# Attention and feed-forward in one kernel: exponentials spread over more slots and tiles, GpSimd's weight work in pieces, one product kept in PSUM

## The chip, the cores and the metric

One NeuronCore of one Trainium2 chip runs the whole kernel. The metric is the device time of one execution in microseconds (us), the median of several runs. "PE" is TensorE, "PEld" its weight loads, "DVE" VectorE, "ACT" ScalarE, "POOL" GpSimd, "SP" the engine whose queue issues the DMAs.

## What is computed

```python
scores = 0.125 * q @ k.T                       # 4 batches, 8 heads, 768 positions, head size 64
keep = (key < n_sink) | ((0 <= query - key) & (query - key < window))   # 4 sinks, window 128
a = softmax(where(keep, scores, -1e9))         # sum + 1e-9 under the fraction
x = (a @ v) laid out as 3072 tokens x 512
h = x @ w_in                                   # 512 -> 2048
g = s * relu(h)**2 + b
out = g @ w_out                                # 2048 -> 512
```

All inputs and the output are float32. `w_in` and `w_out` are drawn with larger factors, so plain bfloat16 isn't used for the products. The kernel splits most operands of its matmuls into a high and a low part of a rounded float32 kind (`float32r`, one pass of TensorE), and multiplies hi by hi, hi by lo and lo by hi.

## The kernel before, in words

The 3072 tokens are eight chunks of 384 (`ORDER`, `CH`). A chunk's attention gives `x`, 512 x 384, as a high and a low tile; its feed-forward part (`moe_steps`) has 16 first products `l1(f)` (L589, 12 matmuls into one PSUM bank `h`) and 16 second ones `l2(f)` (L608, 9 matmuls into three banks `po` that stand through the chunk). While chunk c does its feed-forward, the attention of chunk c+1 is laid between its steps: `slots` are spread evenly over `steps` (last loop of the function). After `l1`, four instructions make `g`: ACT's relu (L592) from PSUM to `r`, DVE's `s*h*r` (L594), ACT's `+ b` rounded to the high part (L596), DVE's low part (L597).

Chunks 0 and 1 are computed by the class `Plain` ("chains" in plain float32), four head pairs each: `scores` (matmuls L491, DVE's mask and maximum L506, ACT's exponential L508, tiles `sm`), `norm` (DVE L513, L514 and six L519, times one over the sum), `turned` in three parts (four transposes each, L531, copied out by ACT, L533), `values` (matmuls L542, copies L544, L545). `plain_slots` puts them into slots: pair `pr` begins at slot 6 pr, `norm` comes `FN` slots later, `turned` `FB`, `values` `FC`; the first number of each holds for chunk 1, the second for chunk 0. Chunk 0 has nothing beside it but the making of weights: it is the kernel's head. Its tiles `sm0` are 8 (`E0`), four for a pair; chunk 1's are taken in turn from three tags of two tiles each.

Weights come as float64 words (1 MB for one f). `make_weight` turns them into float32 parts: ACT L211, L212, DVE L213, L214, GpSimd's add L216, ACT's rounding L220, and the low part L225 on GpSimd for odd f and on DVE for even f. In the head the first pieces are made; in chunk 0's feed-forward `before(f)` makes two more pieces ahead of each `l1(f)`. From chunk 1 on all weights stand in SBUF.

The instructions of an engine don't keep the order of the text. The program's builder orders them anew for each engine by what it takes to be ready (in the trace L149, of a later function, stands ahead of L117); on the chip each engine then runs its own list in order. PSUM has five banks in the pool `psA` (`sc`, `tp` of chunk 1, `o`, `h`) and three in `psO` (`po`, and `tp` of chunk 0). The other chunks' attention (`attn_slots`) uses two tiles `psks`, which `constants2` sets to zero.

Of the kernel before, what the change touches and what calls it, by code (L numbers as in the profile page):

```python
# [6 lines left out]
F32 = mybir.dt.float32  # L7
# [8 lines left out]
P = 128  # L16
# [15 lines left out]
WARM0 = 14  # L32
NARROW, NEARLY = 2, 8
RB, VB = 2, 2
E0 = 8
FN, FB, FC = (4, 2), (6, 6), (9, 10)
LB, LC, LD, L2 = 3, 6, 2, 2


# [1 line left out]
def tile_kernel(ctx, tc, qT, kT, k0, v, vsk, n_sink, window, w, s, b, out):  # L41
# [91 lines left out]
    def constants2():  # L133

        spread = wk.tile([P, P], F32, tag="y", name="spread", bufs=1)
        nc.gpsimd.memset(spread, 0.0)
        for j in range(2):
            nc.gpsimd.affine_select(
                out=spread[96:P].rearrange("p (a d) -> p a d", a=2), in_=spread[96:P].rearrange("p (a d) -> p a d", a=2),
                pattern=[[1, 2], [0, D]], compare_op=ALU.not_equal, fill=1.0, base=2 * j, channel_multiplier=-1)  # L140
        nc.scalar.copy(sel, spread)
        for t in psks:
            nc.gpsimd.memset(t, 0.0)

        nc.vector.tensor_tensor(out=tmp[:, :NS], in0=low[:, :NS], in1=snk[:, :NS], op=ALU.mult)
        nc.vector.tensor_tensor(out=tmp[:, :NS], in0=snk[:, :NS], in1=tmp[:, :NS], op=ALU.subtract)
        nc.vector.scalar_tensor_tensor(out=tm2[:, :NS], in0=rel1[:, :NS], scalar=w_ap, in1=snk[:, :NS],
                                       op0=ALU.is_ge, op1=ALU.mult)
        nc.vector.tensor_scalar(out=split[:, 0, :], in0=rel, scalar1=0.0, scalar2=None, op0=ALU.is_gt)  # L149
        nc.vector.tensor_scalar(out=split[:, 1, :], in0=rel, scalar1=0.0, scalar2=None, op0=ALU.is_le)  # L150
        mask(m_0[:, :NS], tmp[:, :NS])
        mask(m_1[:, 2 * P:], tm2[:, :NS])
        mask(m_even[:, P:P + NS], snk[:, :NS])
        cp = nc.gpsimd.tensor_copy
        upm, lom = m_full[2][:, P:2 * P], m_full[2][:, 2 * P:]
        cp(out=m_0[:, NS:], in_=lom)
        for m, l0 in ((m_1, P), (m_even, P + NS), (m_odd, P)):
            cp(out=m[:, :P], in_=upm)
            cp(out=m[:, l0:l0 + P], in_=lom)
        cp(out=m_odd[:, 2 * P:], in_=m_even[:, P:P + NS])  # L160
# [33 lines left out]
    def piece(f, j, t):  # L194

        n = len(raws[f])
        if n == 1:
            return weight[f][:, :, t, :]
        a = DM * 2 // n
        return weight[f][:, j * 2 // n, t, j * a % DM:j * a % DM + a]  # L200

    def make_weight(j):

        f = j // 2
        if j % 2 == 0 and f < NF:
            for i, raw in enumerate(raws[f]):
                lo, hi = raw[..., 0], raw[..., 1]
                t = scratch(f, i)  # L210
                nc.scalar.activation(lo, lo.bitcast(U32), AF.Copy, scale=2.0 ** -29)  # L211
                nc.scalar.mul(hi.bitcast(F32), hi.bitcast(F32), 2.0 ** -111)  # L212
                nc.vector.tensor_scalar(out=t, in0=hi, scalar1=3, scalar2=None, op0=ALU.logical_shift_left)  # L213
                nc.vector.scalar_tensor_tensor(out=hi, in0=hi, scalar=-0x80000000, in1=t,  # L214
                                               op0=ALU.bitwise_and, op1=ALU.bitwise_or)
                nc.gpsimd.tensor_tensor(out=hi, in0=hi, in1=lo, op=ALU.add)  # L216
        if j % 2 == 1:
            weight[f] = place(f).bitcast(F32R)
            for c, raw in enumerate(raws[f]):
                nc.scalar.copy(piece(f, c, 0), raw[..., 1].bitcast(F32))  # L220
        f -= 1
        if j % 2 == 0 and f >= 0:
            for c, raw in enumerate(raws[f]):
                e = nc.gpsimd if f % 2 == 1 else nc.vector
                e.tensor_tensor(out=piece(f, c, 1), in0=raw[..., 1].bitcast(F32), in1=piece(f, c, 0).bitcast(F32), op=ALU.subtract)  # L225
            raws.pop(f)


# [214 lines left out]
    class Plain:  # L443
# [33 lines left out]
        def scores(self, pr, group):  # L477
# [14 lines left out]
            for i in self.groups[group]:  # L492
                c0, n = (0, P, 0)[i], (i + 1) * P
                for hh in range(2):
                    j = 2 * (i // 2) + hh
                    if pp.sm[j] is None:
                        if self.c:
                            tag = ("kh", "kl", "qs")[self.turn % 3]
                            self.turn += 1
                            pp.sm[j] = wk.tile([P, CH], F32, tag=tag, name="smf")  # L500
                        else:
                            pp.sm[j] = first.tile([P, CH], F32, tag="sm0", name="sm0", bufs=E0)
                    sm = pp.sm[j][:, c0:c0 + n]
                    u = (self.c * H + 2 * pr + hh) * BLK + i
                    uu = slice(u, u + 1)
                    nc.vector.tensor_tensor_reduce(out=sm, in0=banks[(i // 2, hh)][:, c0:c0 + n], in1=m_full[i], scale=-0.125, scalar=BIG,  # L506
                                                   op0=ALU.add, op1=ALU.min, accum_out=negm[:, uu])
                    nc.scalar.activation(sm, sm, AF.Exp, bias=negm[:, uu], scale=-1.0, accum_out=pp.z[:, 0, i, hh:hh + 1])  # L508
# [41 lines left out]
    def plain_slots(c):  # L550
# [6 lines left out]

        first_one = c == 0
        for pr in range(H // 2):
            t = 6 * pr  # L560
            at(t - (0 if first_one else 6), k.load, pr)
            for g in range(len(k.groups)):
                at(t + 2 * g, k.scores, pr, g)
            for part in range(3):
                at(t + FB[first_one] + part, k.turned, pr, part)
            at(t + FN[first_one], k.norm, pr)
            at(t + FC[first_one], k.values, pr)
# [10 lines left out]
    def moe_steps(x, store, wk, before=None, last=False):  # L578
# [3 lines left out]
        def l1(f):  # L582
# [4 lines left out]
            for cc in range(NCC):  # L587
                for wi, xi in ((0, 0), (0, 1), (1, 0)):
# [2 lines left out]
            r = wk.tile([P, CH], F32, tag="r", name="r", bufs=RB)  # L591
            nc.scalar.activation(r, h[:, :CH], AF.Relu, scale=1.0 / WUP)  # L592

            nc.vector.scalar_tensor_tensor(out=r, in0=h[:, :CH], scalar=sw_ap, in1=r, op0=ALU.mult, op1=ALU.mult)  # L594
            gg = wk.tile([P, 2, CH], F32R, tag="g", name="g", bufs=3)
            nc.scalar.activation(gg[:, 0, :], r, AF.Identity, bias=b_ap, scale=1.0)  # L596
            nc.vector.scalar_tensor_tensor(out=gg[:, 1, :], in0=r, scalar=b_ap, in1=gg[:, 0, :].bitcast(F32),  # L597
                                           op0=ALU.add, op1=ALU.subtract)
            g[f] = gg

# [141 lines left out]
    NC_ = 2 * B  # L742
    k, slots = plain_slots(0)
    k.load_first(slice(0, 1))
    nc.sync.dma_start(sb[:, 0:1], s.partition_broadcast(P))
    nc.sync.dma_start(sb[:, 1:2], b.partition_broadcast(P))
    constants()
    k.load_first(slice(1, NCC))
    k.load_values()
    for i, f in enumerate(slots):  # L750
        f()
        if i == 10:
# [7 lines left out]
    late_cm = tc.tile_pool(name="late", bufs=1)  # L760
    late.append(late_cm.__enter__())
    for c in range(NC_):
        steps = moe_steps(k.x, store_at(c), wk, before if c == 0 else None, c == NC_ - 1)
        slots = []
        if c + 1 < NC_:
# [59 lines left out]
```

## Time and profile before

| | us |
|---|---|
| median of 3 runs (lowest, highest) | 745.1 (744.76, 747.49) |
| profiled execution, its own time | 745.48 |
| its span, first to last instruction | 743.7 |
| busy: PE, PEld | 707.4 (95%), 617.5 (83%) |
| busy: DVE, ACT, POOL | 507.5 (68%), 478.7 (64%), 398.2 (54%) |
| mean granted TensorE clock | 0.977 of full speed |

The span is cut into stretches by the windows view; within one, the waits view says who waited for whom, and the timeline gives single instructions. Busy shares over the whole span mix stretches that are unlike each other.

### The profile page before, as it was taken

How to read it: one execution, taken by the hardware profiler on the slowest of the kernel's cores; microseconds unless marked ns; L12 is line 12 of the kernel's file. 1: busy time of each engine (PE TensorE's matmuls, PEld its weight loads, DVE VectorE, ACT ScalarE, POOL GpSimd, SP SyncE). 2: the span in 40 equal slices, each digit the busy share in tenths (PEclk: the TensorE clock that was granted, in tenths of full speed). 3: DMA queues.
4: the chain of work that ended last, by engine and by line, in shares of the span. 5: the costliest groups of instructions: out<-in, count | busy, mean ns of one | idle time of the engine just before them, and what ended most of it. 6: DMA issues, size and time to landing. Idle time of an engine off the chain costs nothing.

```text
span 743.7 us, 11974 instructions
## 1 busy us (share of the span) xinstructions
PE 707.4 (95%) x3848; PEld 617.5 (83%) x3848; DVE 507.5 (68%) x1213; ACT 478.7 (64%) x1169; POOL 398.2 (54%) x641
## 2 busy tenths in 40 slices
PE   6788799999999999999999999999999999999996
PEld 3367577789888998899888998899889999889885
DVE  6779999647874778657776678838776568743231
ACT  4978877567774777656774677738675578643222
POOL 2254654358982789626772589816664379710000
PEclk8889989999999999999999999999999999999999
DMA  7845131042221211111111222112111212001001
GB/s 272 339 169 191 33 115 57 27 126 67 62 65 44 70 56 53 44 64 50 54 49 49 73 67 67 46 40 64 55 52 41 86 42 61 9 1 43 1 0 48
DMA packets 27222, 53.03 MB, mean 71 GB/s; under 512 B 3472, under 2 KB 15376, under 8 KB 25232
## 3 DMA queue, kind: packets, MB, share of 16 engines
q1 hardware_dynamic: 27152, 52.18, 21.0%
q8 instruction: 33, 0.54, 0.3%
q14 instruction: 37, 0.30, 0.1%
HBM read 45.88 MB, written 6.29 MB: 70 GB/s over the span
## 4 chain that ended last, share of the span: by engine, by line
PE 67%; DVE 15%; ACT 6%; DMA 4%; issue 3%; POOL 3%; SPq 1%; ACTq 0%; DVEq 0%; POOLq 0%
PE po L608 29%; PE h L589 28%; PE o L376 2%; DVE g L597 2%; DMA vf<-in_v 2%; PE sc L303 2%; PE sc L304 2%; ACT sm L314 2%; DMA w<-in_w 2%; DVE w L214 2%; PE sc L324 2%; DVE wt L213 1%; POOL w L216 1%; DVE r L594 1%; DVE xm L385 1%
## 5 line engine op out<-in xcount | busy, mean ns | idle before, releaser
L589 PE MATMUL h<-x,w 128*128 128x384 f32 x1536 | 296.2, 342 | 3.5 <-DVE hl L343 2.5
L608 PE MATMUL po<-w,g 128*128 128x512 f32 x1152 | 293.2, 400 | 0.0
L589 PEld LDWEIGHTS h<-x,w 128*128 128x128 f32 x1536 | 268.7, 189 | 10.6 <-DVE hl L343 2.9
L608 PEld LDWEIGHTS po<-w,g 128*128 128x128 f32 x1152 | 211.8, 190 | 45.1 <-issue 2.4
L594 DVE SCALAR_TENSOR_TENSOR r<-h,sb,r 128x384 f32<-128x384 f32 x128 | 78.7, 615 | 68.9 <-ACT r L592 67.9
L597 DVE SCALAR_TENSOR_TENSOR g<-r,sb,g 128x384 fp32r<-128x384 f32 x128 | 92.0, 719 | 42.5 <-ACT g L596 41.5
L596 ACT ACTIVATE g<-r,sb 128x384 fp32r<-128x384 f32 x128 | 78.6, 614 | 52.1 <-DVE r L594 51.8
L340 POOL TENSOR_TENSOR hl<-two,hl 128x256 fp32r<-128x256 f32 x128 | 99.4, 777 | 20.8 <-ACT hl L339 18.1
L592 ACT ACTIVATE r<-h 128x384 f32<-128x384 f32 x128 | 62.5, 489 | 66.2 <-PE h L589 65.8
L314 ACT ACTIVATE sm<-sm,negm 128x272 f32<-128x272 f32 (+1 forms) x144 | 73.1, 508 | 45.7 <-DVE negm L308 43.4
L317 POOL TENSOR_TENSOR sm<-sm 128x128 f32<-128x128 f32 x128 | 65.4, 511 | 57.1 <-ACT sm L314 55.2
L308 DVE CUSTOM_DVE_ANT_0 sm<-sc,msk 128x272 f32<-128x272 f32 (+1 forms) x144 | 60.5, 420 | 47.7 <-PE sc L304 46.2
L284 POOL TENSOR_TENSOR kl<-kraw,kh 128x544 fp32r<-128x544 f32 (+1 forms) x48 | 62.5, 1303 | 24.5 <-ACT kh L282 23.9
L289 POOL TENSOR_TENSOR vv<-vraw,vv 128x256 fp32r<-128x256 f32 (+1 forms) x48 | 39.1, 816 | 38.3 <-ACT vv L288 38.0
L216 POOL TENSOR_TENSOR w<-w 128x1024 int32<-128x1024 int32 (+1 forms) x17 | 32.6, 1920 | 45.6 <-DVE w L214 25.1
L318 POOL COPY psk<-sm 128x48 f32<-128x48 f32 x144 | 40.7, 282 | 29.6 <-ACT sm L314 27.3
L337 DVE TENSOR_TENSOR two<-sc,split 128x256 f32<-128x256 f32 x128 | 53.4, 417 | 2.1 <-POOL hl L340 1.1
L339 ACT CAST hl<-two 128x256 fp32r<-128x256 f32 x128 | 50.2, 392 | 6.2 <-DVE two L337 6.2
L303 PE MATMUL sc<-kh,qs 128*128 128x272 f32 (+1 forms) x144 | 50.8, 355 | 0.0
L385 DVE TENSOR_TENSOR xm<-o,y 64x512 f32<-64x512 f32 x48 | 33.1, 689 | 24.1 <-ACT y L384 14.9
L376 PE MATMUL o<-hl,vv 128*128 128x256 f32 (+1 forms) x256 | 44.4, 275 | 0.0
L283 DVE TENSOR_TENSOR qs<-qraw,qs 64x384 fp32r<-64x384 f32 x48 | 38.3, 798 | 5.1 <-ACT qs L279 3.8
(129 smaller groups left out, 915.0 us busy)
## 6 DMA issues: line engine op xcount, KB each, us to landing
w<-in_w SPq DMA_DIRECT2D x15, 1024.0 KB, 9.1
kraw<-in_kT SPq DMA_DIRECT2D x32, 272.0 KB, 2.6
out<-ot SPq DMA_DIRECT2D x24, 256.0 KB, 2.0
qraw<-in_qT SPq DMA_DIRECT2D x24, 192.0 KB, 2.5
vraw<-in_v SPq DMA_DIRECT2D x16, 256.0 KB, 2.6
kraw<-in_kT SPq DMA_DIRECT2D x16, 208.0 KB, 2.4
vsraw<-in_vsk SPq DMA_DIRECT2D x24, 64.0 KB, 1.9
vraw<-in_v SPq DMA_DIRECT2D x8, 192.0 KB, 2.4
```

Source lines behind the costliest of these rows:

```text
L284: nc.gpsimd.tensor_tensor(out=hd.kl[:, :kw], in0=hd.k[:, :kw], in1=hd.kh[:, :kw].bitcast(F32), op=ALU.subtract)
L303: nc.tensor.matmul(sc[:, :n], hd.qs[:, qs], hd.kh[:, c0:c0 + n], start=True, stop=False)
L308: nc.vector.tensor_tensor_reduce(out=sm[:, :n], in0=sc[:, :n], in1=m, scale=-0.125, scalar=BIG, op0=ALU.add, op1=ALU.min, accum_out=negm[: ...
L314: nc.scalar.activation(sm[:, :n], sm[:, :n], AF.Exp, bias=negm[:, uu], scale=-1.0, accum_out=pp.zz[:, i, hh:hh + 1])
L317: nc.gpsimd.tensor_tensor(out=sm[:, c1:c1 + P], in0=sm[:, p1:p1 + P], in1=sm[:, c1:c1 + P], op=ALU.add)
L340: nc.gpsimd.tensor_tensor(out=lo, in0=both, in1=hi.bitcast(F32), op=ALU.subtract)
L589: nc.tensor.matmul(h[:, :CH], weight[f][:, 0, wi, cc * P:(cc + 1) * P], x[xi][:, cc, :], start=(i == 0), stop=(i == 11))
L592: nc.scalar.activation(r, h[:, :CH], AF.Relu, scale=1.0 / WUP)
L594: nc.vector.scalar_tensor_tensor(out=r, in0=h[:, :CH], scalar=sw_ap, in1=r, op0=ALU.mult, op1=ALU.mult)
L596: nc.scalar.activation(gg[:, 0, :], r, AF.Identity, bias=b_ap, scale=1.0)
L597: nc.vector.scalar_tensor_tensor(out=gg[:, 1, :], in0=r, scalar=b_ap, in1=gg[:, 0, :].bitcast(F32), op0=ALU.add, op1=ALU.subtract)
L608: nc.tensor.matmul(po[tb], gg[:, gi, tsl], weight[f][:, 1, wi, :], start=(f == 0 and i == 0), stop=(f == NF - 1 and i == 2))
```

## The change

The diff, whole. `E0` becomes 16, so each pair of chunk 0 has tiles of its own. `in_parts` issues a GpSimd operation in pieces of at most 256 columns; it is used for L216 and for L225 on GpSimd. The slot numbers become `FN` (3, 2), `FB` (7, 8), `FC` (11, 12), and chunk 1's pairs begin 5 slots apart and load 5 slots ahead. Chunk 1's exponentials take a fourth kind of tile, the two `psks`, which are therefore set to zero only when chunk 1's feed-forward begins. In chunk 0 (`before` is given) L594 writes back into `h`'s bank, and L596 and L597 read it there. In the head the second pair's q and k are loaded by themselves, and the loads of s and b come after the values.

```diff
--- before.py
+++ after.py
@@ -32,8 +32,9 @@
 WARM0 = 14
 NARROW, NEARLY = 2, 8
 RB, VB = 2, 2
-E0 = 8
-FN, FB, FC = (4, 2), (6, 6), (9, 10)
+E0 = 16
+PART = 256
+FN, FB, FC = (3, 2), (7, 8), (11, 12)
 LB, LC, LD, L2 = 3, 6, 2, 2
 
 
@@ -139,9 +140,6 @@
                 out=spread[96:P].rearrange("p (a d) -> p a d", a=2), in_=spread[96:P].rearrange("p (a d) -> p a d", a=2),
                 pattern=[[1, 2], [0, D]], compare_op=ALU.not_equal, fill=1.0, base=2 * j, channel_multiplier=-1)
         nc.scalar.copy(sel, spread)
-        for t in psks:
-            nc.gpsimd.memset(t, 0.0)
-
         nc.vector.tensor_tensor(out=tmp[:, :NS], in0=low[:, :NS], in1=snk[:, :NS], op=ALU.mult)
         nc.vector.tensor_tensor(out=tmp[:, :NS], in0=snk[:, :NS], in1=tmp[:, :NS], op=ALU.subtract)
         nc.vector.scalar_tensor_tensor(out=tm2[:, :NS], in0=rel1[:, :NS], scalar=w_ap, in1=snk[:, :NS],
@@ -199,6 +197,14 @@
         a = DM * 2 // n
         return weight[f][:, j * 2 // n, t, j * a % DM:j * a % DM + a]
 
+    def in_parts(out, in0, in1, op):
+
+        n = out.shape[-1]
+        for c in range(out.shape[1] if len(out.shape) == 3 else 1):
+            for a in range(0, n, PART):
+                q = (slice(None),) + ((c,) if len(out.shape) == 3 else ()) + (slice(a, min(a + PART, n)),)
+                nc.gpsimd.tensor_tensor(out=out[q], in0=in0[q], in1=in1[q], op=op)
+
     def make_weight(j):
 
 
@@ -213,7 +219,7 @@
                 nc.vector.tensor_scalar(out=t, in0=hi, scalar1=3, scalar2=None, op0=ALU.logical_shift_left)
                 nc.vector.scalar_tensor_tensor(out=hi, in0=hi, scalar=-0x80000000, in1=t,
                                                op0=ALU.bitwise_and, op1=ALU.bitwise_or)
-                nc.gpsimd.tensor_tensor(out=hi, in0=hi, in1=lo, op=ALU.add)
+                in_parts(hi, hi, lo, ALU.add)
         if j % 2 == 1:
             weight[f] = place(f).bitcast(F32R)
             for c, raw in enumerate(raws[f]):
@@ -221,8 +227,8 @@
         f -= 1
         if j % 2 == 0 and f >= 0:
             for c, raw in enumerate(raws[f]):
-                e = nc.gpsimd if f % 2 == 1 else nc.vector
-                e.tensor_tensor(out=piece(f, c, 1), in0=raw[..., 1].bitcast(F32), in1=piece(f, c, 0).bitcast(F32), op=ALU.subtract)
+                do = in_parts if f % 2 == 1 else nc.vector.tensor_tensor
+                do(out=piece(f, c, 1), in0=raw[..., 1].bitcast(F32), in1=piece(f, c, 0).bitcast(F32), op=ALU.subtract)
             raws.pop(f)
 
 
@@ -495,9 +501,9 @@
                     j = 2 * (i // 2) + hh
                     if pp.sm[j] is None:
                         if self.c:
-                            tag = ("kh", "kl", "qs")[self.turn % 3]
+                            tag = ("kh", "kl", "qs", "")[self.turn % 4]
+                            pp.sm[j] = wk.tile([P, CH], F32, tag=tag, name="smf") if tag else psks[self.turn // 4 % 2].rearrange("p i c -> p (i c)")
                             self.turn += 1
-                            pp.sm[j] = wk.tile([P, CH], F32, tag=tag, name="smf")
                         else:
                             pp.sm[j] = first.tile([P, CH], F32, tag="sm0", name="sm0", bufs=E0)
                     sm = pp.sm[j][:, c0:c0 + n]
@@ -557,8 +563,8 @@
 
         first_one = c == 0
         for pr in range(H // 2):
-            t = 6 * pr
-            at(t - (0 if first_one else 6), k.load, pr)
+            t = (6 if first_one else 5) * pr
+            at(t - (0 if first_one else 5), k.load, pr)
             for g in range(len(k.groups)):
                 at(t + 2 * g, k.scores, pr, g)
             for part in range(3):
@@ -591,10 +597,11 @@
             r = wk.tile([P, CH], F32, tag="r", name="r", bufs=RB)
             nc.scalar.activation(r, h[:, :CH], AF.Relu, scale=1.0 / WUP)
 
-            nc.vector.scalar_tensor_tensor(out=r, in0=h[:, :CH], scalar=sw_ap, in1=r, op0=ALU.mult, op1=ALU.mult)
+            hr = h[:, :CH] if before else r
+            nc.vector.scalar_tensor_tensor(out=hr, in0=h[:, :CH], scalar=sw_ap, in1=r, op0=ALU.mult, op1=ALU.mult)
             gg = wk.tile([P, 2, CH], F32R, tag="g", name="g", bufs=3)
-            nc.scalar.activation(gg[:, 0, :], r, AF.Identity, bias=b_ap, scale=1.0)
-            nc.vector.scalar_tensor_tensor(out=gg[:, 1, :], in0=r, scalar=b_ap, in1=gg[:, 0, :].bitcast(F32),
+            nc.scalar.activation(gg[:, 0, :], hr, AF.Identity, bias=b_ap, scale=1.0)
+            nc.vector.scalar_tensor_tensor(out=gg[:, 1, :], in0=hr, scalar=b_ap, in1=gg[:, 0, :].bitcast(F32),
                                            op0=ALU.add, op1=ALU.subtract)
             g[f] = gg
 
@@ -742,11 +749,12 @@
     NC_ = 2 * B
     k, slots = plain_slots(0)
     k.load_first(slice(0, 1))
+    constants()
+    k.load_first(slice(1, 2))
+    k.load_first(slice(2, NCC))
+    k.load_values()
     nc.sync.dma_start(sb[:, 0:1], s.partition_broadcast(P))
     nc.sync.dma_start(sb[:, 1:2], b.partition_broadcast(P))
-    constants()
-    k.load_first(slice(1, NCC))
-    k.load_values()
     for i, f in enumerate(slots):
         f()
         if i == 10:
@@ -760,6 +768,9 @@
     late_cm = tc.tile_pool(name="late", bufs=1)
     late.append(late_cm.__enter__())
     for c in range(NC_):
+        if c == 1:
+            for t in psks:
+                nc.gpsimd.memset(t, 0.0)
         steps = moe_steps(k.x, store_at(c), wk, before if c == 0 else None, c == NC_ - 1)
         slots = []
         if c + 1 < NC_:
```

## Rows read from the trace of the kernel before

**Rows 1.** Busy time of each engine in three stretches: the head until the first matmul of the first feed-forward chunk, that chunk, and the rest. Columns: stretch, its length, then busy us and number of instructions for PE, PEld, DVE, ACT and POOL, the granted TensorE clock as a share of full speed, the DMA share and GB/s.

```profile
0.00:45.60 45.60, 30.99 (x158) 16.70 (x158) 32.01 (x121) 31.84 (x75) 14.02 (x26) 0.83 0.65 249
45.60:152.40 106.80, 95.62 (x482) 76.36 (x481) 93.22 (x163) 80.61 (x156) 51.50 (x31) 0.93 0.29 106
152.40:743.70 591.30, 580.76 (x3211) 524.48 (x3210) 382.25 (x929) 366.27 (x939) 332.64 (x584) 1.00 0.17 51
```

**Rows 2.** What TensorE waited for from 0 to 152.4 us: us in total, number of times, longest.

```profile
PE tp L531 <- DVE smf L519: 7.6, 3, 2.9
...
PE o L542 <- ACT tf L533: 7.5, 5, 2.4
...
PE tp L531 <- DVE sm L519: 5.1, 4, 1.9
...
PE h L589 <- ACT tf L533: 1.0, 1, 1.0
```

**Rows 3.** TensorE in order of time in the head: start, length, line, operation, count, and in brackets the idle time before it with what ended it.

```profile
11.64 1.58 PE L491 MATMUL sc<-k,q 64*128 64x128 f32 x12 [3.27 <-DMA k<-in_k]
...
21.28 0.93 PE L491 MATMUL sc<-k,q 64*128 64x128 f32 x8
```

**Rows 4.** DMA issues from 0 to 135 us by line: KB each, median us from issue to landing.

```profile
k<-in_k SPq DMA_DIRECT2D x1, 576.0 KB, 7.5
...
k<-in_k SPq DMA_DIRECT2D x1, 192.0 KB, 3.6
```

**Rows 5.** The SP queue (DMA issues) in order of time: start, time to issue.

```profile
2.61 0.43 SPq L745 DMA_DIRECT2D sb<-in_s  x1
...
4.03 0.49 SPq L457 DMA_DIRECT2D k<-in_k  x1
```

**Rows 6.** ScalarE in order of time in the head, the first exponential of the second head pair.

```profile
12.90 0.40 ACT L508 ACTIVATE sm<-sm,negm 128x128 f32<-128x128 f32 x1 [1.75 <-DVE negm L506]
```

**Rows 7.** VectorE in order of time, chosen instructions: start, length.

```profile
16.89 1.65 DVE L519 TENSOR_SCALAR sm<-sm,zf 128x128 f32<-128x128 f32 x6
...
35.07 1.86 DVE L513 TENSOR_SCALAR zf<-zf 128x6 f32<-128x6 f32 x1
...
37.20 3.81 DVE L519 TENSOR_SCALAR sm<-sm,zf 128x128 f32<-128x128 f32 x6
...
49.87 0.62 DVE L594 SCALAR_TENSOR_TENSOR r<-h,sb,r 128x384 f32<-128x384 f32 x1 [0.66 <-ACT r L592]
...
52.66 2.39 DVE L597 SCALAR_TENSOR_TENSOR g<-r,sb,g 128x384 fp32r<-128x384 f32 x1 [1.07 <-ACT g L596]
...
67.60 0.68 DVE L213 TENSOR_SCALAR wt<-w 128x1024 int32<-128x1024 int32 x1
...
68.31 3.34 DVE L214 SCALAR_TENSOR_TENSOR w<-w,wt 128x1024 int32<-128x1024 int32 x1
...
83.24 0.55 DVE L506 CUSTOM_DVE_ANT_0 smf<-sc,m_all 128x384 f32<-128x384 f32 x1
```

**Rows 8.** GpSimd in order of time, chosen instructions: start, length.

```profile
34.16 2.75 POOL L216 TENSOR_TENSOR w<-w 128x1024 int32<-128x1024 int32 x1 [7.54 <-ACT tf L533]
...
52.19 2.45 POOL L225 TENSOR_TENSOR w<-w,w 128x1024 fp32r<-128x1024 f32 x1 [1.23 <-ACT w L220]
...
67.32 3.25 POOL L225 TENSOR_TENSOR w<-w,w 128x1024 fp32r<-128x1024 f32 x1 [1.24 <-ACT w L220]
...
82.85 2.22 POOL L216 TENSOR_TENSOR w<-w 128x1024 int32<-128x1024 int32 x1
...
131.26 0.74 POOL L225 TENSOR_TENSOR w<-wraw,w 128x256 fp32r<-128x256 f32 x1
...
132.36 0.61 POOL L216 TENSOR_TENSOR wraw<-wraw 128x256 int32<-128x256 int32 x1 [0.36 <-DVE wraw L214]
```

**Rows 9.** Groups of instructions from 45.6 to 152.4 us, shapes kept apart: count, busy us, mean ns of one, idle before them and what ended most of it.

```profile
L597 DVE SCALAR_TENSOR_TENSOR g<-r,sb,g 128x384 fp32r<-128x384 f32 x16 | 18.2, 1140 | 3.7 <-ACT g L596 3.6
...
L594 DVE SCALAR_TENSOR_TENSOR r<-h,sb,r 128x384 f32<-128x384 f32 x16 | 9.8, 612 | 3.3 <-ACT r L592 3.3
...
L214 DVE SCALAR_TENSOR_TENSOR w<-w,wt 128x1024 int32<-128x1024 int32 x10 | 14.3, 1433 | 0.2
...
L216 POOL TENSOR_TENSOR w<-w 128x1024 int32<-128x1024 int32 x10 | 21.7, 2169 | 22.0 <-DVE w L214 9.1 <-ACT r L592 5.3 <-ACT w L220 4.8
...
L225 POOL TENSOR_TENSOR w<-w,w 128x1024 fp32r<-128x1024 f32 x5 | 14.3, 2866 | 8.6 <-ACT w L220 8.6
...
L596 ACT ACTIVATE g<-r,sb 128x384 fp32r<-128x384 f32 x16 | 9.9, 616 | 9.7 <-DVE r L594 9.7
...
L592 ACT ACTIVATE r<-h 128x384 f32<-128x384 f32 x16 | 7.6, 478 | 2.6 <-PE h L589 2.6
...
L542 PE MATMUL o<-tf,vf 128*64 128x384 f32 x16 | 3.5, 512 | 2.5 <-ACT tf L533 2.5
```

**Rows 10.** TensorE in order of time in the first feed-forward chunk.

```profile
68.86 3.37 PE L608 MATMUL po<-w,g 128*128 128x512 f32 x9
...
72.06 2.28 PE L589 MATMUL h<-x,w 128*128 128x384 f32 x12
...
74.53 2.35 PE L608 MATMUL po<-w,g 128*128 128x512 f32 x9
...
96.72 3.13 PE L589 MATMUL h<-x,w 128*128 128x384 f32 x12
```

## The prediction, made before the changed kernel ran

> **What bounds the kernel now.** I read the windows first [rows 1]. After 152.4 us TensorE is busy for 580.8 of 591.3 us at full clock: there the kernel is bound by its matmuls, and nothing in the diff takes one away. What can be won lies ahead of it. In the head (45.6 us) no matmul of the feed-forward runs. In chunk 0's feed-forward (106.8 us) PE is busy for 95.6 us, so 11.2 us idle, at a mean clock of 0.93; two levels, full and half, with that mean cost about 0.07 x 106.8 = 7.5 us more. The floor of this stretch is thus about 106.8 - 18.7 = 88 us. DVE is busy for 93.2 us of it, ACT for 80.6, POOL for 51.5.
>
> Then the waits [rows 2]: TensorE's largest are for the normalised exponentials of DVE, 7.6 us in three stops in chunk 1's chains and 5.1 us in four in the head. So I asked why DVE is late, and put its timeline beside GpSimd's [rows 7, 8]. L597 at 52.66 takes 2.39 us and ends at 55.05; GpSimd's L225 runs from 52.19 to 54.64, and what is left behind it, 0.4 us, is about the instruction itself. L214 at 68.31 takes 3.34 us under the L225 that ends at 70.57. L513, on six columns, takes 1.86 us until L216 ends at 36.91, and the six L519 after it take 3.81 us under L225, where an earlier pair's took 1.65. So most DVE instructions whose tensors are all in SBUF stand still while GpSimd's runs, and everything behind them in DVE's queue with them. One that reads PSUM doesn't: L506 at 83.24 takes 0.55 us in the middle of GpSimd's 82.85 to 85.07. Over the chunk L597 takes 1140 ns on average where L594, of the same shape with `h` in PSUM, takes 612 [rows 9].
>
> **The change part by part.** The sum is made for the profiled execution, 745.48 us, which is 0.4 above the median.
>
> *r in h's bank.* L597 gets a PSUM operand like L594's: 16 x (1140 - 612) = 8.4 us off DVE's 93.2. Part returns, since the next SBUF-only instruction may meet the same GpSimd instruction. What L594 costs when it writes to PSUM no row shows; nearest is the same instruction with the PSUM read, 612 ns, and ACT's L596 from SBUF against L592 from PSUM (616 against 478 ns) gives 0.14 us as the size of such a difference either way, 2.2 us over 16. I take nothing for it. The price is the bank: `h` is held until L597 ends instead of L594. For the first one that is 50.5 to 55.05, 4.6 us, or 2.8 without the stall of 1.8 [rows 7]. With five banks PE waited for one visibly only once, 1.0 us at L589 [rows 2]; I let this become 3.2, a loss of 2.2, with 0 and 16 x 1.0 = 16 as ends.
>
> *Pieces.* GpSimd's add of 256 columns takes 0.61 us and the subtraction 0.74 [rows 8], so a whole add becomes 4 x 0.61 = 2.4 us where one took 2.17 on average; a subtraction becomes 3.0 where it took 2.87 [rows 9]. That is 0.3 us more per add, on an engine that is idle for half of the stretch. In return a DVE instruction waits for the rest of a piece, 0.7 us at most, instead of 2 to 3. GpSimd's result is later, and ACT's rounding L220 waits for it in order, with relu behind it; I take 1.0 us for that (two of the ten adds exposed).
>
> *Slots of chunk 1.* From `norm` to `turned` there are now 4 slots instead of 2 (7 - 3 against 6 - 4), and 28 slots share 106.8 us, 3.8 us each. The extra 7.6 us is more than the longest single stop, 2.9. The fourth tile kind is what lets the next pair's exponentials be written meanwhile: 8 tiles, two whole pairs. I therefore count the 7.6 us as gone, and with them the slow matmuls right behind two stops: 3.37 us against 2.35 for nine, 3.13 against 2.28 for twelve [rows 10], 1.9 us. `values` now stands 2 slots behind the last `turned` (11 - 9), not 1 (9 - 8), so of the 2.5 us for L533 [rows 9] half goes, 1.2. Of the other 5.6 us of slow clock I take 1.5. What is late next is ACT: 80.6 us of work in some 98. Pairs begin 5 slots apart, so q and k of a pair must come in three slots after the one before is read, about 11 us; a load of 192 KB lands in under 4 [rows 4]. `v` waits for the earlier `values`, as it did.
>
> Sum for this stretch: 7.6 + 1.9 + 1.2 + 1.5 - 2.2 - 1.0 = 9.0 us.
>
> *Head.* Pair 1's matmuls begin at 11.64, 3.27 us after PE was free, on a k of 576 KB which takes 7.5 us from 4.03 [rows 3 to 5]. Alone it is 192 KB, which takes 3.6 us, and is issued where b's load stood, half a us behind s's at 2.61: it lands before PE is free. Pair 2's scores start at 21.28 though their k is there at 11.5: with 8 tiles they wait for pair 0's, with 16 they don't. What this brings is set by ACT, idle 1.75 us before pair 1 [rows 6] and then nearly full: I take 2.5 us. Pair 3's chain loses 5.9 us in L513 to L519 from 35.07 where the earlier pair's 1.65 and two short ones ahead make about 2.1, so 3.8 of stall; with pieces two short ones stay (0.61 + 0.74), 2.5 us won. Against it two more issues ahead of the first weight, 0.45 each, and the later slots of `turned` and `values` with one more weight piece ahead of the last: 0.5 us. Sum 4.5 us; ends 0 and 8, the latter if every stop of PE in [rows 3] and the 5.1 of [rows 2] went.
>
> *Nothing:* s and b are loaded behind the values, but first used after the first l1; the two memsets move into chunk 1, where GpSimd is idle for over 40% [rows 1].
>
> Together 9.0 + 4.5 = 13.5: 745.48 - 13.5 = 732.0, less 0.4 to the median, **731.6 us**.
>
> **The rivals.** *All stalls go.* Both stretches reach their floors but for a few us: 16 + 6 = 22, about 723. For it: DVE's stalls feed nearly all PE waits. Against: ACT at over 85% in order. *Half.* DVE back to back meets piece after piece, so the locked time is cut little, and only the slots help: 4 + 2.5 = 6.5, about 738.5. For it: a DVE queue that is 87% full meets GpSimd whenever it works. *GpSimd is shut out* (the slower side). L225 at 67.32 took 3.25 us against 2.4 alone since DVE's L213 at 67.60 went first [rows 7, 8]. In pieces the ten whole adds and five subtractions of the chunk are 40 x 0.61 + 20 x 0.74 = 39 us, and GpSimd's other work there is 51.5 - 21.7 - 14.3 = 15.5, together 55 us. If each of the 60 pieces also waits for a DVE instruction, the weights set the chunk once 55 + 60 w passes it: this way loses from w = 0.94 us (111 us, the 4.5 of the head used up). At 1.0 us, between L594's 0.61 and L214's 1.43 [rows 9], it is 115 us, 8 more than now, and 749; at 1.43 it is 774. Against it: DVE's PSUM reads leave gaps, and GpSimd has 50 us to spare. The Trainium skill (SBUF — State Buffer, "SBUF: two separate sides") calls the shared pair an exclusive lock that whoever starts first holds for the whole instruction; by it each piece may lose once more, which is this rival, and the trace agrees that the wait lasts to the other's end (52.66 to 55.05). *It doesn't do what it says:* the banks held longer return all that DVE wins, 9 us: the head alone, 4.5 less a little, about 742 to 745.
>
> **How the numbers follow.** Forecast (its own range 727 to 736) 0.50, all stalls 0.13, half 0.21, shut out 0.08, banks 0.08. Within 0.5% (3.7 us, what a measurement can tell) is half of the last and a little more. Faster 0.86, same 0.06, slower 0.08. The range of 8 in 10 reaches from 724 into the half case, 741.
>
> **What would show it.** L597's mean in chunk 0 under 0.7 us; no DVE instruction of the chunk stretched by over 0.8; PE's wait for `smf` L519 under 2 us; the first L589 at about 41; the first matmul of chunk 1's feed-forward near 139; the rest 591 us as before. Wrong: L589 or L491 waiting for copies over 3 us in total (banks), or PE waiting for L220 or L225 (GpSimd).

## The result: slower by half a per cent, and the profile after

The changed kernel takes 749.54 us in the median (748.73 to 750.15, 8 runs), the kernel before, measured beside it, 744.93. The ratio is 1.0056, with a 95% interval of 1.0034 to 1.0077. Forecast were 731.6 us and a gain; 749.54 lies above the range, which ended at 741. The profiled execution has a span of 747.8 us.

In `after` the lines move down: L589 is L595, L608 L615, L592 L598, L594 L601, L596 L603, L597 L604, L519 L525, L533 L539, L491 L497, L542 L548; of the weights L213 is L219, L214 L220, L216 L222, L220 L226, L225 L231. GpSimd's pieces all carry L206, the line of `in_parts`.

The same three stretches as in [rows 1], cut again at the first L595 and at the first matmul of chunk 1's feed-forward:

```profile
0.00:43.74 43.74, 30.98 (x159) 17.52 (x159) 34.25 (x122) 33.27 (x77) 16.71 (x36) 0.84 0.66 260
43.74:156.36 112.62, 98.51 (x483) 77.80 (x481) 83.79 (x162) 77.66 (x155) 64.47 (x84) 0.92 0.28 104
156.36:747.80 591.44, 580.64 (x3211) 524.45 (x3209) 381.85 (x929) 367.41 (x939) 332.93 (x584) 1.00 0.16 51
```

The rest takes 591.4 us, as before. The head is 1.9 us shorter (43.7 against 45.6), chunk 0's feed-forward 5.8 us longer (112.6 against 106.8). So the whole loss is in the stretch where the largest gain was forecast. And the engines say something odd about it: DVE, of which I had said that it holds everything up, is busy for 83.8 us instead of 93.2, and yet PE is slower. GpSimd went from 51.5 to 64.5 us. PE itself is busy for 98.5 us instead of 95.6 with about as many matmuls, at a mean granted clock of 0.92 instead of 0.93, and idle for 14.1 instead of 11.2: only half of the 5.8 us is idle time.

What PE waits for in that stretch, to be read against [rows 2]:

```profile
PE h L595 <- ACT tf L539: 5.0, 2, 4.6
PE sc L497 <- DVE g L604: 5.0, 3, 3.1
PE o L548 <- ACT tf L539: 1.9, 2, 1.6
PE tp L537 <- DVE negm L512: 1.5, 1, 1.5
PE h L595 <- DVE g L604: 0.7, 1, 0.7
```

No wait for normalised exponentials is left, where there were three stops of 7.6 us in all. In their place stand waits for ACT's copies `tf` and for DVE's L604, which frees `h`'s bank: 5.0, 5.0, 1.9 and 0.7 us, and 1.5 for a maximum (L512). Together these are 14.1 us; before, the three stops and the 2.5 and 1.0 us for `tf` [rows 2, 9] made 11.1, so the stops moved and grew by 3.0. `tf` and L604 are written by instructions that wait themselves; one step further back is what ACT waits for in the same stretch, first in the kernel before and then in the changed one:

```profile
ACT g L596 <- DVE r L594: 9.7, 8, 2.7
ACT w L220 <- POOL w L216: 4.7, 6, 1.6
ACT w L220 <- DVE w L225: 2.8, 2, 1.7
```

The same view of the changed kernel:

```profile
ACT w L226 <- POOL w L206: 20.9, 9, 3.9
ACT r L598 <- PE h L595: 5.4, 3, 3.1
...
ACT w L226 <- DVE w L231: 2.5, 1, 2.5
```

ACT now stands at L226, the rounding of a weight, for GpSimd: 20.9 us in place of 4.7. An engine runs its list in order, so relu, `g` and the copies `tf` behind L226 stand with it. One such stop on three engines, ACT, GpSimd, PE (the number in brackets is the idle time before):

```profile
120.96 0.44 ACT L218 ACTIVATE wraw<-wraw 128x256 f32<-128x256 f32 x1
123.54 0.66 ACT L226 CAST w<-w 128x512 fp32r<-128x512 f32 x1 [2.14 <-POOL w L206]
124.10 0.49 ACT L598 ACTIVATE r<-h 128x384 f32<-128x384 f32 x1
126.75 0.67 ACT L226 CAST w<-w 128x512 fp32r<-128x512 f32 x1 [2.17 <-POOL w L206]
127.32 0.58 ACT L539 COPY tf<-tp 128x512 f32<-128x512 f32 x1
```

GpSimd in the same timeline (start in us, duration, engine, line, operation):

```profile
121.69 3.45 POOL L206 TENSOR_TENSOR w<-w 128x256 int32<-128x256 int32 x4
125.11 1.61 POOL L206 TENSOR_TENSOR w<-w,w 128x256 fp32r<-128x256 f32 x2
```

And PE's two instructions on either side of its stop:

```profile
122.77 0.60 PE L537 MATMUL tp<-identr,smf 128*128 128x128 f32 x4
127.95 4.21 PE L595 MATMUL h<-x,w 128*128 128x384 f32 x12 [4.59 <-ACT tf L539]
```

ACT reaches L226 at 121.4 and waits until the last of GpSimd's adds it needs is done, at 123.5; then at 124.6 it waits for the next, until GpSimd has done its subtraction, 126.7. Why a rounding waits for a subtraction stands in the kernel: `load_weight` puts the raw words of weight f, for all but the last, into the tile of weight f + 1, L231 reads them there, and the rounding of weight f + 1 writes over them, so it must come later. Three of the nine stops, 9.1 us, end with a subtraction. The copy `tf` at 127.32 is behind both. PE needs that copy's bank for its next L595 and has idled since 123.4; and then the twelve matmuls take 4.2 us, at half clock (granted 0.50 from 127.95 to 132.2), instead of 2.3.

Why GpSimd is late is in the groups, to be read against [rows 9]:

```profile
L206 POOL TENSOR_TENSOR w<-w 128x256 int32<-128x256 int32 x48 | 35.9, 775 | 28.0 <-DVE w L220 16.5 <-ACT w L218 7.6 <-ACT r L598 2.4
...
L206 POOL TENSOR_TENSOR w<-w,w 128x256 fp32r<-128x256 f32 x24 | 19.8, 854 | 6.3 <-ACT w L226 6.3
...
L601 DVE SCALAR_TENSOR_TENSOR h<-h,sb,r 128x384 f32<-128x384 f32 x16 | 9.9, 621 | 8.0 <-ACT r L598 8.0
L604 DVE SCALAR_TENSOR_TENSOR g<-h,sb,g 128x384 fp32r<-128x384 f32 x16 | 9.8, 616 | 6.2 <-ACT g L603 6.1
L603 ACT ACTIVATE g<-h,sb 128x384 fp32r<-128x384 f32 x16 | 9.3, 581 | 0.9 <-DVE h L601 0.9
```

L604 takes 616 ns where L597 took 1140: with a PSUM operand DVE isn't stopped here (all sixteen took 605 to 619 ns; L597 took 606 to 2786). L601, which now writes to PSUM, takes 621 against 612. But four pieces of an add take 4 x 775 = 3.1 us, where the whole add took 2.17; four of a subtraction 3.4, where it took 2.87. A piece alone takes 0.61 or 0.74 [rows 8]; the rest I put down to waiting for DVE, piece by piece, while DVE waits for GpSimd, instruction by instruction. Here both are slow at once:

```profile
62.74 3.71 DVE L525 TENSOR_SCALAR smf<-smf,zf 128x128 f32<-128x128 f32 x5
```

GpSimd's timeline in the changed kernel over the same time:

```profile
61.94 3.67 POOL L206 TENSOR_TENSOR w<-w,w 128x256 fp32r<-128x256 f32 x4 [1.73 <-ACT w L226]
```

GpSimd's four pieces take 3.67 us, and DVE's five normalisations beside them 3.71.

### The profile page after: what moved, and what is told of

It is laid out like the page before. It is cut to its first block, busy times and chain, and to the rows that moved or that the text cites. A ratio compares the mean times of both kernels' runs of the same rounds, so it can differ in the third digit from the quotient of the medians.

```text
span 747.8 us, 12047 instructions
## 1 busy us (share of the span) xinstructions
PE 710.1 (95%) x3848; PEld 619.8 (83%) x3848; DVE 499.9 (67%) x1213; ACT 478.3 (64%) x1169; POOL 414.1 (55%) x704
## 4 chain that ended last, share of the span: by engine, by line
PE 71%; DVE 9%; ACT 9%; POOL 7%; issue 3%; DMA 0%; ACTq 0%; DVEq 0%; POOLq 0%
PE h L595 29%; PE po L615 29%; POOL w L206 6%; PE o L382 3%; PE sc L309 2%; PE sc L310 2%; PE sc L330 2%; ACT sm L320 1%; DVE xm L391 1%; DVE sm L314 1%; ACT w L218 1%; PE zb L410 1%; PE tp L537 1%; ACT w L217 1%; DVE qs L289 1%
## 5 line engine op out<-in xcount | busy, mean ns | idle before, releaser
L595 PE MATMUL h<-x,w 128*128 128x384 f32 x1536 | 296.8, 342 | 8.2 <-ACT tf L539 5.0
L615 PE MATMUL po<-w,g 128*128 128x512 f32 x1152 | 294.2, 401 | 0.0
L595 PEld LDWEIGHTS h<-x,w 128*128 128x128 f32 x1536 | 268.6, 189 | 15.4 <-ACT tf L539 5.8
L615 PEld LDWEIGHTS po<-w,g 128*128 128x128 f32 x1152 | 212.7, 190 | 45.4 <-issue 2.1
L346 POOL TENSOR_TENSOR hl<-two,hl 128x256 fp32r<-128x256 f32 x128 | 99.6, 778 | 20.9 <-ACT hl L345 18.4
L601 DVE SCALAR_TENSOR_TENSOR r<-h,sb,r 128x384 f32<-128x384 f32 x112 | 68.9, 615 | 61.5 <-ACT r L598 60.4
L598 ACT ACTIVATE r<-h 128x384 f32<-128x384 f32 x128 | 62.8, 490 | 71.0 <-PE h L595 70.6
L320 ACT ACTIVATE sm<-sm,negm 128x272 f32<-128x272 f32 (+1 forms) x144 | 73.2, 508 | 46.5 <-DVE negm L314 44.2
L604 DVE SCALAR_TENSOR_TENSOR g<-r,sb,g 128x384 fp32r<-128x384 f32 x112 | 73.1, 652 | 38.0 <-ACT g L603 36.9
L603 ACT ACTIVATE g<-r,sb 128x384 fp32r<-128x384 f32 x112 | 68.8, 614 | 41.9 <-DVE r L601 41.5
L206 POOL TENSOR_TENSOR w<-w 128x256 int32<-128x256 int32 x60 | 44.3, 768 | 34.1 <-DVE w L220 16.5
```

The costliest lines, as they stand in the source:

```text
L206: nc.gpsimd.tensor_tensor(out=out[q], in0=in0[q], in1=in1[q], op=op)
L320: nc.scalar.activation(sm[:, :n], sm[:, :n], AF.Exp, bias=negm[:, uu], scale=-1.0, accum_out=pp.zz[:, i, hh:hh + 1])
L346: nc.gpsimd.tensor_tensor(out=lo, in0=both, in1=hi.bitcast(F32), op=ALU.subtract)
L595: nc.tensor.matmul(h[:, :CH], weight[f][:, 0, wi, cc * P:(cc + 1) * P], x[xi][:, cc, :], start=(i == 0), stop=(i == 11))
L601: nc.vector.scalar_tensor_tensor(out=hr, in0=h[:, :CH], scalar=sw_ap, in1=r, op0=ALU.mult, op1=ALU.mult)
L603: nc.scalar.activation(gg[:, 0, :], hr, AF.Identity, bias=b_ap, scale=1.0)
```

## The experiments

Eighteen kernels are compared here, two of them the kernels before and after. In the table head and stretch are read from the windows of each run's profiled execution, cut as above; DVE and POOL are their busy us within the stretch. One profiled execution can lie off the median of its kernel: that of d_pieces took 747.38 us, that of d_slots 746.13. The kernel before was measured again beside each group (medians 744.19 to 745.01), and the ratio is to those runs; it is not the quotient of two medians of the table. The rest, from chunk 1's feed-forward on, took 590.9 to 592.1 us in every one.

| kernel | median us | ratio to before (95%) | head | stretch | DVE | POOL |
|---|---|---|---|---|---|---|
| before | 744.93 | | 45.6 | 106.8 | 93.2 | 51.5 |
| after | 749.54 | 1.0056 (1.0034 to 1.0077) | 43.7 | 112.6 | 83.8 | 64.5 |
| u_pieces | 748.13 | 1.0035 (1.0012 to 1.0059) | 45.8 | 108.5 | 92.2 | 50.6 |
| u_bank | 746.81 | 1.0016 (0.9994 to 1.0038) | 43.6 | 109.5 | 86.8 | 71.3 |
| u_slots | 750.47 | 1.0059 (1.0040 to 1.0078) | 43.6 | 114.3 | 80.3 | 66.6 |
| u_head | 748.00 | 1.0020 (0.9999 to 1.0042) | 44.0 | 110.8 | 82.8 | 71.2 |
| u_pb | 747.93 | 1.0050 (1.0030 to 1.0069) | 46.0 | 109.0 | 96.8 | 51.4 |
| d_pieces | 744.32 | 0.9989 (0.9968 to 1.0009) | 46.3 | 107.7 | 87.2 | 71.8 |
| d_bank | 744.82 | 0.9996 (0.9976 to 1.0016) | 46.8 | 106.0 | 90.8 | 50.4 |
| d_slots | 748.17 | 1.0048 (1.0016 to 1.0081) | 43.8 | 109.6 | 90.0 | 54.6 |
| e_short | 734.27 | 0.9872 (0.9855 to 0.9888) | 41.4 | 99.2 | 75.0 | 36.6 |
| d_short | 734.31 | 0.9868 (0.9839 to 0.9897) | 39.7 | 102.2 | 82.2 | 27.7 |
| e_sub | 743.47 | 0.9990 (0.9975 to 1.0004) | 44.2 | 106.3 | 84.2 | 47.0 |
| e_sub_whole | 739.49 | 0.9931 (0.9908 to 0.9954) | 43.4 | 102.5 | 88.0 | 35.0 |
| d_sub | 740.00 | 0.9931 (0.9891 to 0.9971) | 42.0 | 104.0 | 92.4 | 35.4 |
| d_sub_bank | 741.15 | 0.9935 (0.9895 to 0.9974) | 45.7 | 101.8 | 92.7 | 33.7 |
| u_pb_sub | 738.66 | 0.9903 (0.9871 to 0.9935) | 44.1 | 103.6 | 89.6 | 35.6 |
| e_sw_oldslots | 737.62 | 0.9886 (0.9846 to 0.9926) | 43.6 | 100.1 | 88.6 | 33.8 |

The head alone differs by several us between executions: d_sub and d_sub_bank have the same order on PE, ACT, DVE and GpSimd up to the first `l1`, and heads of 42.0 and 45.7 us. So a difference of less than 4 us in one head or one stretch is at most a hint; whole times go by the runs.

**One part undone, from the changed kernel.**

u_pieces:

```diff
-                in_parts(hi, hi, lo, ALU.add)
+                nc.gpsimd.tensor_tensor(out=hi, in0=hi, in1=lo, op=ALU.add)
...
-                do = in_parts if f % 2 == 1 else nc.vector.tensor_tensor
+                do = (nc.gpsimd if f % 2 == 1 else nc.vector).tensor_tensor
```

> The changed kernel with GpSimd's L206 issued whole again; the order of the instructions on PE, ACT, DVE and SP stays as in the changed kernel. Theory P (pieces are what costs: an add in pieces lasts 3.1 us instead of 2.2, and ACT's list stands at L226 for it, 23.5 us in the trace of the changed kernel against 4.7 before): ACT's wait at L226 falls under 10 us, time 738 to 743. Theory B (h's bank held longer, PE waits 5.7 us for L604) and theory S (the new slots and the order they give): 747 to 752, since DVE's stalls behind whole instructions come back.

u_bank:

```diff
-            hr = h[:, :CH] if before else r
+            hr = r
```

> The changed kernel with r in SBUF again in chunk 0; PE's order stays as in the changed kernel. Theory B: PE's waits for L604 (5.7 us) go, 742 to 745. Theory P: ACT's wait at L226 stays near 23 us, L597 meets pieces, 748 to 752. Theory S: as P.

u_slots:

```diff
-FN, FB, FC = (3, 2), (7, 8), (11, 12)
+FN, FB, FC = (4, 2), (6, 8), (9, 12)
...
-            t = (6 if first_one else 5) * pr
+            t = 6 * pr
...
-                            tag = ("kh", "kl", "qs", "")[self.turn % 4]
+                            tag = ("kh", "kl", "qs")[self.turn % 3]
```

> The changed kernel with chunk 1's slot numbers, its spacing of 6 and its three tags as before. Theory S: 739 to 744. Theory P: ACT's wait at L226 stays over 18 us and PE's wait for normalised exponentials comes back, 749 to 755. Theory B: 747 to 752.

u_head:

```diff
-E0 = 16
+E0 = 8
...
-FN, FB, FC = (3, 2), (7, 8), (11, 12)
+FN, FB, FC = (3, 2), (7, 6), (11, 10)
...
-    k.load_first(slice(1, 2))
-    k.load_first(slice(2, NCC))
+    k.load_first(slice(1, NCC))
```

> The changed kernel with the head of before (8 tiles, turned and values two slots earlier, the loads in their old order). All three theories: the first L589 is at 45 to 46 instead of 43.7, and the time 750 to 752. If the head's new order is what harms chunk 0's feed-forward: 745 to 748.

No part, undone, takes the whole loss away, and each theory missed where its own part was undone. u_pieces keeps the order of PE, ACT, DVE and SP, so it is the cleanest: its stretch is 4.1 us shorter than after's, but its head longer, and 748.13 is a part of the way at most, where theory P had 738 to 743; PE's stop for `tf` near 125 us stays, 3.5 us. ACT's wait for GpSimd at L226 is 14.0 us, not under 10:

```profile
ACT w L226 <- POOL w L222: 8.7, 4, 2.7
ACT w L226 <- POOL w L231: 5.3, 3, 3.0
```

u_bank, 746.81, lies above theory B's range and below that of the others; all its ten runs (746.31 to 748.33) lie below all eight of after, so in this order the bank costs some 2.7 us. u_head, 748.00, has a head of 44.0, not of 45 to 46. u_bank and u_head come nearest to before, 1.0016 and 1.0020, but the intervals of all three overlap after's. In u_slots PE's 7.6 us of stops at normalised exponentials are back and the stretch is 1.7 us longer; 750.47 lies in the ranges of theories P and B, and theory S, which expected a gain, falls. That left the question whether the parts harm alone.

**One part alone, from the kernel before**, and the head and the slots together (u_pb, which is the changed kernel with both edits of u_pieces and that of u_bank). d_pieces, d_bank and d_slots add to the kernel before what u_pieces, u_bank and u_slots take from the changed one; in all three the zeroing of psk stands in chunk 1.

> The changed kernel without pieces and without r in h's bank: head and slots alone are new. If what the two cost in chunk 0's feed-forward adds up (4.1 us from u_pieces, 3.1 from u_bank, against 112.6): stretch 105.4, with a head of 45.8 about 744.5. If both act through the same stop (ACT stands at L226, so L603 and L604 are late and h's bank with them), they don't add up: stretch 108, about 747.

> The kernel before with GpSimd's pieces alone (and the zeroing of psk moved). Its order on PE, DVE and SP is that of before. Theory P (the longer GpSimd chain costs in any order): chunk 0's stretch 110 to 111, head 43.7, 746 to 748. Theory I (pieces harm only in the new order, where L226 stands earlier in ACT's list): ACT's wait at L226 under 9 us, stretch 104 to 106, 740 to 743.

> The kernel before with r in h's bank alone. Theory B (a bank held longer costs in any order): PE waits over 3 us for L604, 747 to 749. Theory I (DVE's 8 us are won, and the bank is short only with the new slots' 8 tiles): PE waits under 1 us for L604, 740 to 743.

> The kernel before with chunk 1's slots, spacing and fourth kind of tile alone. Theory N: PE's waits for normalised exponentials go and 741 to 743. Theory S (the new order moves the wait from the exponentials to the banks and ACT's copies): stretch 107 to 109, 746 to 749, PE waiting over 4 us for tf.

Pieces alone change nothing that is measured (0.9989), and neither does the bank alone (0.9996): theory P and theory B fall in the order of before, and so does theory I, which wanted gains of 2 us and more. In d_bank PE waits for L604 for 0.2 us only, as theory I had it. In d_pieces ACT stands at L226 for GpSimd for 16.4 us, without loss:

```profile
ACT w L226 <- POOL w L206: 16.4, 12, 2.8
```

The slots alone are slower, 1.0048, as theory S had it, and with the head 1.0050: u_pb, with 109.0 and 747.93, came out where pieces and bank don't add up. What PE waits for in d_slots:

```profile
PE h L595 <- POOL w L231: 3.9, 1, 3.9
PE o L548 <- ACT tf L539: 2.5, 1, 2.5
PE h L595 <- ACT tf L539: 2.4, 2, 1.6
PE h L595 <- ACT w L226: 2.2, 1, 2.2
PE po L615 <- DVE g L604: 1.2, 1, 1.2
```

The stops at the exponentials are gone there too, and 12.2 us of others stand, where all stops before were 11.1: for a weight's low part (L231), for its high part (L226), for ACT's copies, and 1.2 for L604. PE is now stopped by weights that aren't made yet. So the suspect became the making of weights, and GpSimd's part of it.

**GpSimd's add taken nearly away**, in the changed kernel (e_short) and in the one before (d_short, the same edit on the same line). Both leave out the addition beyond the first 16 columns of each half.

```diff
-                in_parts(hi, hi, lo, ALU.add)
+                nc.gpsimd.tensor_tensor(out=hi[..., :16], in0=hi[..., :16], in1=lo[..., :16], op=ALU.add)
```

> The changed kernel with GpSimd's add done on the first 16 columns of each half only, the rest of the addition left out; the subtractions stay in pieces. The order on PE is that of the changed kernel, on ACT and DVE a few instructions move. If ACT's standing at L226 for GpSimd is what costs: its wait falls from 21 to under 9 us, PE's wait for ACT's tf copies under 1.5 us, time 739 to 743. If h's bank costs by itself: PE's wait for L604 stays at 4 to 5 us, 746 to 749.

> The kernel before with GpSimd's add on the first 16 columns only, the rest of the addition left out. Theory G (GpSimd's conversion chain, add, ACT's L226 and what stands behind it, sets chunk 0 in both kernels, and the change lengthened it): 732 to 737, near e_short's 734.3. Theory N (the new slots and the freed DVE are worth what was forecast, and only the longer chain hid it): 739 to 743, clearly above e_short, with PE still waiting 5 us or more for normalised exponentials.

Both fall to the same 734.3 us, for e_short 4.7 us below the range expected. With the add away, 15 us come back in the changed kernel and 10 to 11 in the one before, and the two are equal: the time is as theory G had it, and theory N, by which the new slots and the freed DVE would then be worth 5 us or more, falls. In the profiled executions they are less alike: e_short gains 2.3 us in the head and 13.4 in the stretch, d_short 5.9 and 4.6. And ACT's wait for GpSimd in d_short is twice that of before, 4.7 us, in a kernel that is 10 us faster:

```profile
ACT w L220 <- POOL w L216: 9.2, 6, 2.1
```

So that wait shows where the chain runs, but not what it costs. PE's waits in d_short and then in e_short:

```profile
PE tp L531 <- DVE smf L519: 2.3, 2, 1.7
PE h L589 <- DVE r L594: 2.2, 1, 2.2
PE h L589 <- ACT x L544: 1.4, 1, 1.4
```

The same view of e_short:

```profile
PE h L595 <- ACT tf L539: 3.7, 2, 3.1
PE sc L497 <- DVE g L604: 1.7, 2, 1.1
```

d_short still has 2.3 us of stops at the exponentials where e_short has none, and its time is the same. PE's wait for `tf` in e_short is 3.7 us, where under 1.5 was expected. What the add costs by its own length and what by holding up DVE these two runs don't part: both fall away with it.

**The subtractions off GpSimd**, every L225 on DVE: from the changed kernel with the adds in pieces (e_sub) and whole (e_sub_whole).

```diff
-                do = in_parts if f % 2 == 1 else nc.vector.tensor_tensor
+                do = nc.vector.tensor_tensor
```

> The changed kernel with every subtraction L225 on DVE; the adds stay on GpSimd in pieces. The order on PE moves by 32 lines. Theory G: ACT's wait at L226 falls from 21 to 12 us or less, since add and subtraction no longer stand one behind the other on GpSimd, and the time to 738 to 744. If DVE's freed time is already used up: DVE busy over 92 us in the stretch, 747 to 751.

> As e_sub, with the adds whole. Theory G with the lock: DVE is stretched by whole adds again, ACT's wait at L226 is shortest of the full kernels (under 8 us); 738 to 744, within 3 us of e_sub. If the pieces are what helps DVE: 4 us or more above e_sub.

743.47 and 739.49: both lower than after, the second lower than before too, 0.9931. e_sub's time is in the range of theory G, but ACT's wait for GpSimd at L226 fell to 14.9 us only, and with 7.2 for the subtraction on DVE it stands there for 22.1, as in after (23.4), in a stretch 6.3 us shorter. e_sub_whole computes everything, with DVE busier than in after (88.0 against 83.8 us) and GpSimd at 35.0 instead of 64.5. Its ACT stands at L226 for GpSimd for 7.8 us instead of 20.9, with 8.3 for the subtraction on DVE in place of 2.5:

```profile
ACT w L226 <- DVE w L231: 8.3, 3, 4.5
ACT w L226 <- POOL w L222: 7.8, 5, 2.7
```

What PE still waits for in the same run is nearly all weights:

```profile
PE h L595 <- DVE w L231: 7.9, 6, 2.6
PE o L548 <- ACT tf L539: 1.1, 1, 1.1
```

e_sub and e_sub_whole have the same order on PE, ACT, DVE and SP; that e_sub_whole is 4 us lower, with no run in common (737.43 to 740.78 against 741.78 to 744.36), says that here the pieces cost by themselves. At most 3 had been expected. Against after the stretch of e_sub_whole is 10.1 us shorter; 5.8 of these are PE's busy time (92.7 us against 98.5, mean granted clock 0.98 against 0.92) and 4.3 its stops: part of what stops cost lies in slower matmuls.

**What is left of the bank and the slots once GpSimd's chain is short.** d_sub is the kernel before with that one edit, d_sub_bank the same with r in h's bank; u_pb_sub is e_sub_whole without the bank, e_sw_oldslots e_sub_whole with the three lines of u_slots.

```diff
-                e = nc.gpsimd if f % 2 == 1 else nc.vector
+                e = nc.vector
```

> The kernel before with every subtraction L225 on DVE and nothing else. Theory G: GpSimd's chain is shorter in any order, stretch 103 to 105, 740 to 743. If only the freed DVE of the changed kernel can take the subtractions: DVE busy near 98 us, 745 to 750.

> d_sub with r in h's bank. If the bank pays once GpSimd's chain is short: 1.5 to 4 us under d_sub, 737 to 740. If not: within 1.5 us of d_sub.

> e_sub_whole (739.5) without r in h's bank. If the bank pays once GpSimd's chain is short: 742 to 746, with L604 at 1000 ns or more. If not: 738 to 741.

> e_sub_whole (739.5) with chunk 1's old slots, spacing and tags. If the new slots pay once GpSimd's chain is short (PE's stops at normalised exponentials come back): 742 to 746. If not: 737 to 741.

The one line of d_sub gives 0.9931, in theory G's range; in its profiled execution 3.6 us of the gain lie in the head and 2.8 in the stretch. The bank adds nothing to be seen in either order (741.15 against 740.00; 739.49 against 738.66 without it), though the stretch alone is 2.2 and 1.1 us shorter with it, less than executions differ by, and the new slots nothing either: with the old ones it is 737.62 against 739.49, the lowest of the complete kernels, intervals overlapping. PE's waits in e_sw_oldslots:

```profile
PE tp L537 <- DVE smf L525: 4.3, 5, 1.5
PE h L595 <- DVE w L231: 2.5, 2, 1.3
```

The stops at the exponentials are there, 4.3 us, and cost nothing that is measured.

## Why the prediction was wrong, by its steps

**What bounds.** That all that can be won lies ahead of 152.4 us was right: the rest is 591 to 592 us in every run. That DVE, held up by GpSimd, is what PE waits for in chunk 0 was the reading of the waits, and it was wrong. It is the step that failed first. PE's stops at L519 are real, but taking them away or relieving DVE won nothing (d_slots 1.0048, d_bank 0.9996), and with 4.3 us of them back the kernel was no slower (e_sw_oldslots). What moved the time most was GpSimd's part in the making of weights: with the add nearly away both orders take 734.3; with the subtractions moved off GpSimd 740.0 and 739.5, though DVE is busy for about as long in d_sub as before (92.4 against 93.2) and for longer in e_sub_whole than in after. Over all eighteen kernels the stretch goes with GpSimd's busy time: 99 to 104 us where that is 28 to 37, 106 to 110 where it is 47 to 55, 108 to 114 where it is 64 to 72. The reading is that the making of weights sets the stretch (ACT, DVE, GpSimd's add, ACT's rounding, the low part, and then the rounding of the next weight), and that stops that end inside that chain's time are slack. The path from GpSimd to PE through ACT's list is argued, not shown: ACT's wait at L226 doesn't follow the time (16.4 us in d_pieces without loss, 9.2 in d_short with a gain, 7.1 in u_pb with the loss of after).

**Slots of chunk 1**, 7.6 + 1.9 + 1.2 + 1.5 us: "I therefore count the 7.6 us as gone." The stops did go, in after and in d_slots; the time did not. PE came to weights and copies that were not ready, 12.2 us of stops in d_slots against 11.1 in all before, and d_slots is 0.5% slower. I named ACT as what is late next, but took its 80.6 us of work in 98 as a cover, and didn't ask what it waits for in its own list. A row that points there, 4.7 us at L220 for GpSimd in the kernel before, was not among those I used.

**r in h's bank.** L597 to L604 fell to 616 ns, under the 0.7 us that I had set, and L601's writing to PSUM cost nothing (621 ns), as taken. The 8.4 us won on DVE were off the path: d_bank 0.9996. The price, 2.2 us for banks, was right in kind and too small in the new order: PE waits 5.7 us for L604 in after, and without the bank the time was some 2.7 us lower (u_bank); in the order of before the wait is 0.2 (d_bank). In e_short, with the new slots and the bank but GpSimd quick, it is 1.7. The sign that I had set for banks, over 3 us of waiting for copies at L589, came too, 5.0 us.

**Pieces**, 1.0 us: GpSimd's pair of an add and a subtraction takes 3.1 + 3.4 us, 1.5 more than the whole ones, where I had 0.4; ACT's wait for GpSimd at L226 grew by 16 us, where I had 1 us of loss. Against u_pieces the stretch is 4.1 us longer, the median 1.4. That is the term that was mis-sized; in the order of before the same pieces cost nothing that is measured (d_pieces); why there was room for ACT's 16.4 us there wasn't tried.

**Head**, 4.5 us: 1.9 came in the profiled execution, and even that isn't shown: without the two kernels whose add is cut short, the heads with the new text last 43.4 to 46.0 us and those with the old 42.0 to 46.8. Pair 1's scores follow pair 0's at once, as said, but the time goes back in two stops of 4.2 us:

```profile
6.98 3.60 PE L497 MATMUL sc<-k,q 64*128 64x128 f32 x24
...
25.35 2.83 PE L548 MATMUL o<-tf,v 128*64 128x384 f32 x12 [4.23 <-ACT tf L539]
...
36.84 0.30 PE L537 MATMUL tp<-identr,sm 128*128 128x128 f32 x1 [4.25 <-DVE sm L525]
```

The one at 25.35 is for copies that stand in ACT's list behind pair 2's exponentials. What the head's parts are worth singly wasn't settled.

**The rivals.** "GpSimd is shut out" had 0.08 and the right place and direction. That its 749 us is what was measured is luck: it is the price at w = 1.0 us, and a piece lasted only 0.11 to 0.17 us longer than alone (854 and 775 ns against 0.74 and 0.61). Its point of decision was wrong: I let it lose only when GpSimd's work fills the stretch, 55 + 60 w over 111 us. GpSimd is busy for 64.5 us of 112.6 in after, far from full; what I take to count is how long one add and one subtraction take while others stand for them. The rule of the Trainium skill beside it (SBUF — State Buffer, "SBUF: two separate sides": a lock for a whole instruction, the loser blocks) agrees with the two rows at 62 us, where both engines are stretched, to 3.67 and 3.71 us; none of my terms but this rival let both sides lose. "Half" and "all stalls go" fall with the reading of the bound; the banks rival, 742 to 745, had the wait right and no loss.

**What stays open.** Why u_slots, with pieces and the bank, is the slowest of all (114.3), and why u_pb loses about as much as after with a third of its wait for GpSimd at L226 (7.1 against 20.9 us): there ACT stands for DVE's L601 instead, 13.3 us. How much of the add's 10 to 15 us is its length and how much its hold on DVE wasn't parted.

## What to carry to other kernels

A stop of the busiest engine names who was late, not who sets the pace. Before a stop is taken away, follow the producers of everything that the engine needs next, here the weights, through every engine's list; if that chain is just in time, the stop is slack. An engine that is half idle can be what a stretch hangs on: GpSimd was busy for 48% of it, and taking work off it was what helped. The quickest test is to leave that work out and see what the kernel then takes. Cutting GpSimd's instructions into pieces relieved DVE (87.2 us busy against 93.2, d_pieces) and cost GpSimd (71.8 against 51.5), with no gain in time; moving the work off the engine (one line, d_sub, 0.7%) was worth more than all edits of the change together.

## What the runs showed of the hardware

In these runs a VectorE instruction with one operand in PSUM was not held up by GpSimd even when it also wrote to PSUM (621 ns) or read a second operand from SBUF (616 ns against 1140 with both in SBUF). ACT's pass over the same shape takes 581 ns from PSUM and took 616 from SBUF. A piece of GpSimd's add, 256 columns, took 0.61 us alone and 0.78 on average beside a busy DVE.
